# The end of a convolution layer: row order, early weights' pieces, and a product with adding transfers

## The chip, the cores and the metric

The kernel runs on one core of a Trainium2 chip. Its engines work side by side, each through its own queue in order: TensorE (PE in the profile; PEld its weight loads), VectorE (DVE), ScalarE (ACT), GpSimd (POOL) and SyncE (SP), which here issues transfers only. The metric is the device time of one launch in microseconds (us), the median of several runs; lower is better.

## The reference

A network of four layers on a sequence of 2048 positions and 640 channels. Layers one and three are a layer norm and a long convolution (a state space kernel, applied by FFT), layers two and four a layer norm and an attention with 32 query heads of 20 channels that share one key and value head. Each adds to the stream.

```python
def _A_ref(u, A_re, A_im, B_re, B_im, C_re, C_im, log_dt, Dskip):
    ...
    K = jnp.einsum("dn,dnl,dn->dl", Cc, P, dB).real
    ...
    Yf = Uf * Kf[None, :, :, :]
    y = irfft2(Yf, ...)[:, :, 0, :L]
    y = y.transpose(0, 2, 1) + u * Dskip[None, None, :]

def _B_ref(x, wq, wk, wv, wo):
    q = (x @ wq).reshape(B, S, H, Dh).transpose(0, 2, 1, 3)
    k, v = x @ wk, x @ wv
    p = _softmax(jnp.einsum("bhqd,bkd->bhqk", q, k) * (Dh ** -0.5))
    return o.transpose(0, 2, 1, 3).reshape(B, S, H * Dh) @ wo

x = A_u
x = x + _A_ref(_layernorm(x), ...)
x = x + _B_ref(_layernorm(x), ...)
x = x + _A_ref(_layernorm(x), ...)
x = x + _B_ref(_layernorm(x), ...)
```

## The kernel before

`tile_layers` runs a generation of the convolution kernels (`kgen`), then `conv_layer("a")`, `attn_layer("b")`, `conv_layer("c")` and `attn_layer("d")`. The stream x (2048 x 640) stays in SBUF as a tile of 128 partitions by 16 rows ("tau") by 640 channels. A row here is one tau: 128 positions by 640 channels. `TAUS` lists the 16 rows in four groups of four, by the order in which the inverse transform gives them.

**A convolution layer** goes through the channels in five chunks of 128 (`c` = 0 to 4). A chunk is normalised on ScalarE (L818), transformed by matmuls with a table of cosines and sines (L652, `raw` and `dense`), then by butterflies of length 8 on VectorE (`whole`, `fft8`, L114 and L117, with scratch B). The spectrum, `A[c]`, holds 16 rows of 256, real parts in the even rows and imaginary parts in the odd ones. It is multiplied by the spectrum of the convolution kernel (`kh`, 2 MB, loaded by SP per chunk, L762), goes through butterflies again and through the inverse matmuls with a table `wi` (L860), four groups g of four rows. An inverse writes one of two PSUM banks (`ps1`), so the third needs the bank of the first, read out. `turn(g)` reads out group g with the addition to x (`residual`: on VectorE at L871, for chunks 0 and 3 on ScalarE at L869, where TensorE has added x itself with an identity matmul, L853) and for g < 2 issues the inverse of group g + 2.

Chunks 0 to 3 are multiplied by `spread`: products in halves of 1024 elements on VectorE (L926, L922, L929, L931), whose sums are made by transfers with addition, issued on POOL's queue (L923, L927). Chunk 4, the last, is multiplied by `product`, six instructions of 2048 elements on VectorE (L837), and goes through `fft8_last`, which gives the inputs of groups 0 and 1 first, in the tile of kh, named K there (the trace calls it Akh), and those of groups 2 and 3 in A (L157, L160). Calls on other engines are woven between these instructions by `weave(calls, between)`, at index numbers of the list: the turns of chunk 3 at 1, 2, 4 and 5 and the weights' pieces at 3 + k and 5 + k.

**The weights' pieces** exist in layer a only. The projection weights are split into a high and a low part (wh, wl), six pieces: k = 0 for wk and wv, k = 1 to 5 for 128 rows of wq each. `first(k)` loads a piece (L1031), rounds it on ScalarE (L1036) and forms the rest on TensorE (L1038, L1040) in one of three PSUM tiles of two banks (`ps2`), `second(k)` writes the rest out on ScalarE (L1045); after the last, wh and wl are stored (L1048) for layer d's use, where layer c loads them.

**The next norm.** The statistics of channels 0 to 383 of all rows are taken on ScalarE during chunk 3 (`stats_first`, L692 to L696, scratch in the tile xn, named xnas or xncs), those of channels 384 to 639 on VectorE when the last chunk's residual of a group is done (`stats_last`, L708, L710). `stats_base` (L701) and `norm_part` (L724 to L731, with `root`, L736 to L741) merge them: first for group 0, then for groups 1 to 3. The root is on ScalarE, the rest on VectorE. All of this from the last `turn(0)` on is outside the block of `manual_schedule`, so that a planner orders it, by program order and estimated times; within such a block the order on the named engines is that of the program.

**The attention layer** begins with `prepare(0)`: four rows of the first block are normalised on ScalarE (L1105, tiles x), transposed on TensorE (L1114), split into xh on ScalarE (L996) and xl on VectorE (L999), in three steps of two, two and one column blocks. `project` multiplies them by wh and wl (L1131), 15 matmuls for each of six parts. Its tiles lie in the memory that the convolution layer frees, tile by tile: a tile waits for the last reader of what lay there. At the same point POOL clears vt, ones and kt (L1075 to L1082), and VectorE casts ob (L1086).

Of the kernel before, what the change touches and what calls it, by code (L numbers as in the profile page):

```python
# [11 lines left out]
F32 = mybir.dt.float32  # L12
# [135 lines left out]
def fft8_last(nc, A, B, R, K):  # L148
# [13 lines left out]
    tt(A[:, 0:8], B[:, 0:8], B[:, 8:16], ADD)  # L162
# [6 lines left out]
    tt(A[:, 8:16], B[:, 0:8], B[:, 8:16], SUB)  # L169
# [24 lines left out]
class Net:  # L194
# [508 lines left out]
    def stats_last(self, g):  # L703

        nc = self.nc
        st = self.xp.tile([P, 4, 6], F32, tag="st", bufs=2, name=f"sl{g}")
        for n in range(4):
            nc.vector.bn_stats(st[:, n], self.x[:, TAUS[4 * g + n], NA:D])  # L708
        for n in range(4):
            nc.vector.bn_aggr(self.mvb[:, 4 * g + n], st[:, n])  # L710
# [5 lines left out]
    def norm_part(self, g, n):  # L716
# [7 lines left out]
        tt(ed, shift, mean, ALU.add)  # L724
        stt(ve, var, PB, base, op0=ALU.mult, op1=ALU.add)
        stt(sq, ed, PA * PB, ed, op0=ALU.mult, op1=ALU.mult)
        stt(nm, ed, -PB, shift, op0=ALU.mult, op1=ALU.add)
        tt(ve, ve, sq, ALU.add)
        rs = self.rs[:, gs]
        self.root(ve, sq, rs)  # L730
        tt(self.nmr[:, gs], nm, rs, ALU.mult)  # L731

    def root(self, ve, sq, out):

        nc = self.nc
        nc.scalar.activation(sq, ve, AF.Sqrt)  # L736
        nc.vector.reciprocal(out, sq)
        nc.vector.tensor_tensor(sq, out, out, ALU.mult)
        nc.vector.tensor_tensor(sq, sq, ve, ALU.mult)
        nc.vector.tensor_scalar(sq, sq, -0.5, 1.5, ALU.mult, ALU.add)  # L740
        nc.vector.tensor_tensor(out, out, sq, ALU.mult)  # L741

    def norm(self, nm, g):
# [10 lines left out]
        self.root(ve, sq, rs)  # L754
# [35 lines left out]
    def conv_layer(self, nm, first):  # L790
# [7 lines left out]
        with tc.manual_schedule(engines={mybir.EngineType.PE, mybir.EngineType.Activation,  # L798
# [37 lines left out]
            def product(A, kh):  # L836
                return [lambda a=a: tt(*a) for a in (  # L837
                    (m(B, 0), m(A, 0), m(kh, 0), ALU.mult),
                    (R, m(A, 1), m(kh, 1), ALU.mult),
                    (m(B, 0), m(B, 0), R, ALU.subtract),  # L840
                    (m(B, 1), m(A, 0), m(kh, 1), ALU.mult),
                    (R, m(A, 1), m(kh, 0), ALU.mult),
                    (m(B, 1), m(B, 1), R, ALU.add))]
# [22 lines left out]
            def residual(c, g, y):  # L866
# [5 lines left out]
                if c == NCH - 1:  # L872
                    self.stats_last(g)
# [65 lines left out]
            for c in range(NCH):  # L939
                A = As.pop(c)  # L940
                if c == NCH - 1:
                    late = [(1, lambda turn=turn: turn(0)), (2, lambda turn=turn: turn(1)),
                            (4, lambda turn=turn: turn(2)), (5, lambda turn=turn: turn(3))]
                    late = sorted(late + [(3 + k, a[0]) for k, a in enumerate(pieces)]
                                  + [(5 + k, a[1]) for k, a in enumerate(pieces)], key=lambda a: a[0])
                    K = khs.pop(c)
                    weave(product(A, K) + fft8_last(nc, A, B, R, K), late)
                else:
# [10 lines left out]
                    if c == NCH - 2:  # L959
                        scr = new_xn("s").rearrange("p a d -> p (a d)")  # L960

                        def dump(n):
                            return scr[:, 1280 + NA * (n % 4) : 1280 + NA * (n % 4) + NA]

                        self.stats_setup(nm)
                        for g in range(4):
                            self.stats_first(g, dump)
                        pieces = self.attn_weights(scr, nm == "a")
# [9 lines left out]
        turn(0)  # L978
        self.stats_base()
        self.norm_part(0, 1)  # L980
        for g in range(1, 4):
            turn(g)
        self.norm_part(1, 3)
# [8 lines left out]

    def split(self, hi, lo, src, act=False):
        nc = self.nc
        if act:
            nc.scalar.activation(hi, src, AF.Copy)  # L996
        else:
            nc.vector.tensor_copy(hi, src)
        nc.vector.tensor_tensor(lo, src, hi.bitcast(F32), ALU.subtract)  # L999

    def attn_weights(self, scr, fresh):
# [17 lines left out]
        minus = scr[:, 2816:2944]  # L1019
# [6 lines left out]
        def first(k):  # L1026
            hi = ends(k)[0]
            pw = pws[k] = self.ps2(f"pw{k}")
            if k:
                src = scr[:, D * (k % 2) : D * (k % 2) + D]  # L1030
# [39 lines left out]
    def _attn(self, ctx, nm, out):  # L1070
# [20 lines left out]
        with tc.tile_pool(name=f"pj{nm}", bufs=1, reuse_waits="tile") as pj:  # L1091
# [5 lines left out]
            xhs, xls = {}, {}  # L1097
# [370 lines left out]
```

## Time and profile before

| | us |
|---|---|
| median of 3 runs | 3002.05 (3000.38 to 3004.14) |
| profiled execution | 2999.59 |
| its span | 2997.8 |
| busy: TensorE, ScalarE, VectorE | 2777.6, 2426.4, 1378.1 |
| last chunk of layer a: first instruction of `product` to first projection matmul | 571.43 to 620.26 |
| the same of layer c | 1876.83 to 1923.07 |

The profile is that of one execution. Its page gives sums per engine and per group of instructions; the answers of the trace give the instructions in order of time. A row of the timeline reads: start, length, engine, line of the kernel, operation, written tile <- read tiles, shapes, how many were merged; in brackets the idle time of the engine just before it, and what ended it. Start times are us from the span's start. TensorE's granted clock is 0.956 of full speed on the mean.

### The profile page before, as it was taken

The numbers are of one execution on the slowest core, as the hardware profiler recorded it, in microseconds if no ns is written. First come the engines' busy times: TensorE is split into PE (matmuls) and PEld (weight loads), VectorE is DVE, ScalarE is ACT, GpSimd is POOL, SyncE is SP. The second block draws the span as 40 slices with busy tenths as digits, with TensorE's granted clock in tenths as the row PEclk, the third lists the DMA queues.
The fourth block names the chain that finished last, engine by engine and source line by source line (L and its number), as shares of the span: only waits on it lengthen the run. The fifth ranks groups of instructions, "written<-read, shape, count | busy, mean of one in ns | idle before, by whom it ended". The sixth has DMA issues, their size and how long they took to land. (4 is left out here: it accounts for less than half of the span.)

```text
span 2997.8 us, 52536 instructions
## 1 busy us (share of the span) xinstructions
PE 2777.6 (93%) x21712; PEld 1269.2 (42%) x21712; DVE 1378.1 (46%) x1794; ACT 2426.4 (81%) x2904; POOL 86.7 (3%) x149
## 2 busy tenths in 40 slices
PE   2776989898999999999999998898999999999999
PEld 0333978775232333232333687772233333333333
DVE  7999899942122332322232599722222322222222
ACT  5888243444999999999999634338999999999997
POOL 0001001000000000000000011000000000000000
PEclk9855999999999999999999999899999999999999
DMA  6113555433200000001000256131001101110100
GB/s 145 34 19 100 186 162 113 104 114 113 81 22 25 22 25 22 27 21 28 21 26 20 87 113 160 39 129 51 22 25 26 39 21 28 38 26 24 41 19 23
DMA packets 126000, 175.60 MB, mean 59 GB/s; under 512 B 59460, under 2 KB 81988, under 8 KB 122132
## 3 DMA queue, kind: packets, MB, share of 16 engines
q1 hardware_dynamic: 102680, 137.70, 15.8%
q0 software_dynamic: 21104, 33.45, 5.5%
q8 instruction: 175, 2.87, 0.4%
q10 hardware_dynamic: 1968, 0.98, 0.1%
q14 instruction: 73, 0.60, 0.1%
HBM read 95.22 MB, written 48.04 MB: 48 GB/s over the span
## 5 line engine op out<-in xcount | busy, mean ns | idle before, releaser
L1264 ACT ACTIVATE pt<-scb 128x1024 f32<-128x1024 f32 x1024 | 942.2, 1113 | 6.7 <-PE scb L1260 5.1
L1264 ACT ACTIVATE pt<-scd 128x1024 f32<-128x1024 f32 x1024 | 942.1, 1115 | 5.8 <-DMA qpd<-mxd 3.9
L1274 PE MATMUL pob<-pt,vt 128*32 128x512 f32 x4096 | 546.6, 606 | 4.4 <-DVE on L1291 0.2
L1274 PE MATMUL pod<-pt,vt 128*32 128x512 f32 x4096 | 546.3, 605 | 4.4 <-DVE on L1291 0.2
L1260 PE MATMUL scb<-qpb,kt 62*128 62x512 f32 x2048 | 385.8, 451 | 6.0 <-DVEq L1209 5.6
L1260 PE MATMUL scd<-qpd,kt 62*128 62x512 f32 x2048 | 385.4, 451 | 5.6 <-DVEq L1209 5.2
L1260 PEld LDWEIGHTS scb<-qpb,kt 62*128 62x128 f32 x2048 | 166.0, 185 | 401.4 <-ACT pt L1264 392.0
L1260 PEld LDWEIGHTS scd<-qpd,kt 62*128 62x128 f32 x2048 | 165.8, 184 | 401.1 <-ACT pt L1264 392.2
L1322 DVE TENSOR_TENSOR x<-pyd,x 128x320 f32<-128x320 f32 x146 | 71.8, 491 | 560.9 <-PE pyd L1334 560.9
L1322 DVE TENSOR_TENSOR x<-pyb,x 128x320 f32<-128x320 f32 x146 | 71.8, 492 | 547.4 <-PE pyb L1334 547.4
L1294 DVE RECIPROCAL rc<-rc 128x512 f32<-128x512 f32 x62 | 207.9, 3353 | 2.1
L1274 PEld LDWEIGHTS pob<-pt,vt 128*32 128x32 f32 x4096 | 80.6, 108 | 178.1 <-issue 160.0
L1274 PEld LDWEIGHTS pod<-pt,vt 128*32 128x32 f32 x4096 | 80.6, 108 | 177.6 <-issue 159.5
L1334 PE MATMUL pyb<-wo,ot 128*32 128x320 f32 x1168 | 105.3, 432 | 0.0
L1334 PE MATMUL pyd<-wo,ot 128*32 128x320 f32 x1168 | 105.3, 432 | 0.0
L652 PE MATMUL za<-xna,wf 128*128 128x256 f32 x384 | 87.4, 390 | 5.0 <-ACT xna L818 5.0
L652 PE MATMUL zc<-xnc,wf 128*128 128x256 f32 x384 | 85.8, 385 | 5.0 <-ACT xnc L818 5.0
L860 PE MATMUL ya<-Aa,wi 128*128 128x128 f32 x576 | 71.8, 289 | 15.5 <-DVE Aa L114 15.5
L1291 DVE COPY on<-pod 128x512 f32<-128x512 f32 x31 | 21.4, 691 | 134.6 <-PE pod L1274 120.6
L1291 DVE COPY on<-pob 128x512 f32<-128x512 f32 x31 | 21.4, 691 | 133.0 <-PE pob L1274 110.0
L443 PE MATMUL pe<-kg,tm 48*128 48x512 bf16 (+1 forms) x120 | 60.1, 603 | 23.9 <-ACT m L451 15.4
L652 PEld LDWEIGHTS za<-xna,wf 128*128 128x128 f32 x384 | 74.8, 196 | 16.8 <-ACT xna L818 6.2
(367 smaller groups left out, 3204.2 us busy)
## 6 DMA issues: line engine op xcount, KB each, us to landing
Akh<-kh SPq DMA_DIRECT2D x10, 2048.0 KB
kh<-Ak SPq DMA_DIRECT2D x5, 2048.0 KB
qhd<-qh SPq DMA_DIRECT2D x40, 256.0 KB
qld<-ql SPq DMA_DIRECT2D x40, 256.0 KB
qpb<-qhd SPq DMA_DIRECT2D x256, 40.0 KB
qpd<-qhd SPq DMA_DIRECT2D x256, 40.0 KB
ot<-on SPq DMA_DIRECT2D x216, 40.0 KB
wf<-in_c_wf POOLq DMA_DIRECT2D x16, 512.0 KB, 7.9
```

The source lines that it names most:

```text
L443: nc.tensor.matmul(pe[:, 512 * h : 512 * h + 512], grp(tm, u, par, rows), kg[0:rows, col : col + 512], start=True, stop=True)
L652: nc.tensor.matmul(zv[:, :, c, kk], self.wf[:, t + 4 * h, j, c, kk], x, start=(n == 0), stop=(n == 3))
L860: nc.tensor.matmul(y[:, s * DC : (s + 1) * DC], self.wi[:, t, j, c_, kk], v[:, 2 * t + c_, kk], start=(i == 0 and not whole), stop=(i == 3 ...
L1260: nc.tensor.matmul(sc[:, 512 * par : 512 * par + 512], kt[rows, 128 * t : 128 * t + 128], qps[nb, hg, pr][rows], start=True, stop=True)
L1264: nc.scalar.activation(pt, sc, AF.Exp, scale=SCALE)
L1274: nc.tensor.matmul(po[32 * j : 32 * j + 32], vt[:, t], pts[step, j // 2][:, 512 * (j % 2) : 512 * (j % 2) + 512], start=(t == 0), stop=(t ...
L1291: nc.vector.tensor_copy(on, po)
L1294: nc.vector.reciprocal(rc, rc)
L1322: nc.vector.tensor_tensor(xh, py, xh, ALU.add)
L1334: nc.tensor.matmul(py[j : j + m], o[:, 128 * i + j : 128 * i + j + m], w[:, 320 * half : 320 * half + 320], start=start, stop=stop)
```

## The change

It does these things:

- `product` takes the imaginary part first, in two halves of 1024 elements: A1 x K0 into B1, A0 x K1 into R, and a transfer with addition on POOL's queue adds R to B1. Then the real part: A0 x K0 into B0, A1 x K1 in place into K1, the difference into B0. Six whole instructions become four halves and three wholes: one of VectorE's six lengths is left out.
- `fft8_last` begins with the even rows (real parts), sum and difference, then the sum of the odd rows; the difference of the odd rows stays behind K.
- In layer a the pieces 0 to 3 are issued ahead of `stats_first` and so ahead of chunk 3's inverses, their second steps between the groups of `stats_first`; the pieces 4 and 5 stay woven in, at 6 to 9. Sources take three places in the scratch instead of two, dumps two instead of four.
- From the last chunk's `turn(0)` on, the order is written out (the block of `manual_schedule` goes on): `turn(0)` ahead of the last two butterflies, then `stats_base`, the statistics of group 0, the first half of its norm, `turn(1)`, the statistics of group 1 with the second half of that norm woven in, and so on. `norm_part` and `root` return lists of calls.
- `prepare(0)` of the attention is in a written order too: the norm of groups 1 to 3 stands on VectorE and ScalarE around the first xl. The tile xh of block 0 is allocated first, ahead of the tiles x, and xh has two names instead of two buffers of one name.

```diff
-    tt(A[:, 0:8], B[:, 0:8], B[:, 8:16], ADD)
+    tt(A[:, 0:8:2], B[:, 0:8:2], B[:, 8:16:2], ADD)
+    tt(A[:, 8:16:2], B[:, 0:8:2], B[:, 8:16:2], SUB)
+    tt(A[:, 1:8:2], B[:, 1:8:2], B[:, 9:16:2], ADD)
     tt(R[:, 0:4], A[:, 0:4], A[:, 4:8], ADD)
...
-    tt(A[:, 8:16], B[:, 0:8], B[:, 8:16], SUB)
+    tt(A[:, 9:16:2], B[:, 1:8:2], B[:, 9:16:2], SUB)
...
             def product(A, kh):
-                return [lambda a=a: tt(*a) for a in (
+                calls = []
+                for h in range(2):
+                    s = slice(4 * h, 4 * h + 4)
+
+                    def imag(s=s):
+                        tt(R[:, s], m(A, 0)[:, s], m(kh, 1)[:, s], ALU.mult)
+                        nc.gpsimd.dma_start(m(B, 1)[:, s], R[:, s], accum_op=ALU.add)
+
+                    calls += [lambda s=s: tt(m(B, 1)[:, s], m(A, 1)[:, s], m(kh, 0)[:, s], ALU.mult), imag]
+                return calls + [lambda a=a: tt(*a) for a in (
                     (m(B, 0), m(A, 0), m(kh, 0), ALU.mult),
-                    (R, m(A, 1), m(kh, 1), ALU.mult),
-                    (m(B, 0), m(B, 0), R, ALU.subtract),
-                    (m(B, 1), m(A, 0), m(kh, 1), ALU.mult),
-                    (R, m(A, 1), m(kh, 0), ALU.mult),
-                    (m(B, 1), m(B, 1), R, ALU.add))]
+                    (m(kh, 1), m(A, 1), m(kh, 1), ALU.mult),
+                    (m(B, 0), m(B, 0), m(kh, 1), ALU.subtract))]
...
-                    late = sorted(late + [(3 + k, a[0]) for k, a in enumerate(pieces)]
-                                  + [(5 + k, a[1]) for k, a in enumerate(pieces)], key=lambda a: a[0])
+                    late = sorted(late + [(6 + k, a[0]) for k, a in enumerate(pieces[4:])]
+                                  + [(8 + k, a[1]) for k, a in enumerate(pieces[4:])], key=lambda a: a[0])
                     K = khs.pop(c)
-                    weave(product(A, K) + fft8_last(nc, A, B, R, K), late)
+                    calls = product(A, K) + fft8_last(nc, A, B, R, K)
+                    weave(calls[:-2], late)
...
                         self.stats_setup(nm)
+                        pieces = self.attn_weights(scr, first)
+                        for a in pieces[:4]:
+                            a[0]()
                         for g in range(4):
                             self.stats_first(g, dump)
-                        pieces = self.attn_weights(scr, nm == "a")
+                            for a in pieces[max(g - 1, 0) : (0, 1, 2, 4)[g]]:
+                                a[1]()
...
-        turn(0)
-        self.stats_base()
-        self.norm_part(0, 1)
-        for g in range(1, 4):
-            turn(g)
-        self.norm_part(1, 3)
+            turn(0)
+
+            for call in calls[-2:]:
+                call()
+            self.stats_base()
+            for g in range(4):
+                if g > 0:
+                    turn(g)
+                among = part[6:] if g == 1 else ()
+                weave(self.stats_last(g), [(min(n + 1, 8), a) for n, a in enumerate(among)])
+                if g == 0:
+                    part = self.norm_part(0, 1)
+                    for call in part[:6]:
+                        call()
...
-                src = scr[:, D * (k % 2) : D * (k % 2) + D]
+                src = scr[:, D * (k % 3) : D * (k % 3) + D]
...
-            xhs, xls = {}, {}
+            xhs, xls = {0: pj.tile([P, 5, 512], F32R, tag="xh0", bufs=1, name="xh0")}, {}
...
-                xh = xhs[nb] = pj.tile([P, 5, 512], F32R, tag="xh", bufs=2, name=f"xh{nb}")
+                if nb > 0:
+                    xhs[nb] = pj.tile([P, 5, 512], F32R, tag=f"xh{nb % 2}", bufs=1, name=f"xh{nb}")
+                xh = xhs[nb]
...
-                    self.split(xh[:, k0 : k0 + n], xl[:, k0 : k0 + n],
-                               pt[:, 0 : 512 * n].rearrange("p (k c) -> p k c", k=n), act=True)
+                    hi, lo = xh[:, k0 : k0 + n], xl[:, k0 : k0 + n]
+                    pv = pt[:, 0 : 512 * n].rearrange("p (k c) -> p k c", k=n)
+                    nc.scalar.activation(hi, pv, AF.Copy)
+
+                    def low(hi=hi, lo=lo, pv=pv):
+                        nc.vector.tensor_tensor(lo, pv, hi.bitcast(F32), ALU.subtract)
+
+                    weave([low], [(0 if n < 6 else 1, a) for n, a in enumerate(
+                        self.norm_part(1, 3) if nb == k0 == 0 else ())])
...
-            prepare(0)
+            with tc.manual_schedule(engines={mybir.EngineType.Activation, mybir.EngineType.DVE}):
+                prepare(0)
```

52 lines of the change are left out of this document (22 added, 30 removed).

## The prediction

> **What bounds the kernel now.** First the page, for the span; then the timeline of each engine around the place that the diff touches.
>
> ```profile
> span 2997.8 us, 52536 instructions
> ```
>
> The two convolution layers (tiles named a and c) end with the last channel chunk, and behind each stands an attention layer whose projections keep TensorE busy from then on. So what counts is when the first projection matmul starts. The timeline of VectorE at the end of layer a (start, length, line, tile, number of instructions), at the product, at the butterflies and at the first residual:
>
> ```profile
> 571.43 2.29 DVE L837 TENSOR_TENSOR B<-Aa,Akh 128x2048 f32<-128x2048 f32 x1
> 573.64 2.29 DVE L837 TENSOR_TENSOR Ra<-Aa,Akh 128x2048 f32<-128x2048 f32 x1
> ```
> ```profile
> 587.33 2.36 DVE L157 TENSOR_TENSOR Ra<-Aa 128x1024 f32<-128x1024 f32 x2
> 589.61 2.49 DVE L157 TENSOR_TENSOR Akh<-Ra 128x512 f32<-128x512 f32 x4
> 592.02 2.28 DVE L157 TENSOR_TENSOR Aa<-B 128x2048 f32<-128x2048 f32 x1
> 594.34 2.50 DVE L157 TENSOR_TENSOR B<-Aa 128x512 f32<-128x512 f32 x4
> ```
> ```profile
> 598.19 2.50 DVE L160 SCALAR_TENSOR_TENSOR Aa<-B 128x512 f32<-128x512 f32 x4
> 600.61 0.68 DVE L871 TENSOR_TENSOR x<-ya,x 128x512 f32<-128x512 f32 x1
> 601.39 1.41 DVE L708 BATCH_NORM_STATS2 sl<-x 128x6 f32<-128x256 f32 x4
> 602.72 0.36 DVE L710 BATCH_NORM_AGGREGATE mvba<-sl 128x2 f32<-128x6 f32 x4
> ```
>
> No row names idle time: VectorE runs through. The inputs of the first two inverses (Akh) are there from 590.2 (the first of four instructions) to 592.1. TensorE's timeline, and further down the first projection:
>
> ```profile
> 595.22 1.25 PE L1040 MATMUL pw<-wh,xnas 128*128 128x512 f32 x4
> 596.30 7.31 PE L860 MATMUL ya<-Akh,wi 128*128 128x128 f32 x64
> 603.45 7.31 PE L860 MATMUL ya<-Aa,wi 128*128 128x128 f32 x64
> ```
> ```profile
> 620.26 0.43 PE L1131 MATMUL pqb<-xh,wh 128*52 128x512 f32 x1 [1.35 <-DVE xl L999]
> ```
>
> It stands in the weights' pieces (pw) until 596.30, 6 us past its first input. The four inverses then take 14.46 us, and ScalarE waits for their end:
>
> ```profile
> 610.85 0.92 ACT L1105 ACTIVATE x<-x,nmrna,rsna 128x640 f32<-128x640 f32 x1 [5.21 <-PE ya L860]
> 613.86 0.21 ACT L736 ACTIVATE sq<-ve 128x12 f32<-128x12 f32 x1 [2.09 <-DVE ve L728]
> 613.98 2.53 ACT L1105 ACTIVATE x<-x,nmrna,rsna 128x640 f32<-128x640 f32 x3
> 617.92 2.43 ACT L996 ACTIVATE xh<-ptb 128x1024 fp32r<-128x1024 f32 x3 [1.42 <-PE ptb L1114]
> ```
>
> One normalised row comes out, then the root for the other twelve stands in front of the next three. In layer c there are no pieces; the same places there, on VectorE, TensorE, ScalarE and TensorE:
>
> ```profile
> 1895.02 2.49 DVE L157 TENSOR_TENSOR Akh<-Rc 128x512 f32<-128x512 f32 x4
> ```
> ```profile
> 1902.57 0.69 DVE L871 TENSOR_TENSOR x<-yc,x 128x512 f32<-128x512 f32 x1 [0.33 <-PE yc L860]
> ```
> ```profile
> 1895.81 10.30 PE L860 MATMUL yc<-Akh,wi 128*128 128x128 f32 x64 [6.49 <-issue]
> ```
> ```profile
> 1913.34 0.92 ACT L1105 ACTIVATE x<-x,nmrnc,rsnc 128x640 f32<-128x640 f32 x1 [3.00 <-PE yc L860]
> ```
> ```profile
> 1923.07 0.43 PE L1131 MATMUL pqd<-xh,wh 128*52 128x512 f32 x1 [1.09 <-DVE xl L999]
> ```
>
> The starts to beat are 620.26 and 1923.07.
>
> **The change, part by part.** *Product.* Before, from 571.43 to the first Akh at 589.61: 18.18 us. After: four halves of 1.14 (half of the R pair's 2.28) are 4.56; then 2.21 (start to start, independent), 2.29 and 2.29: 11.35. Even rows' sum and difference 2.28, odd rows' sum 1.14, R pair 2.28: 17.05. Akh starts 1.13 us earlier: 588.48 in a, 1893.89 in c. One 2.29 us instruction goes, but the difference of the even rows now stands ahead of Akh. Behind it: Akh 2.41, odd difference 1.14, six butterflies 3.85 (594.34 to 598.19), two of the four L160 1.21: the first residual 8.61 after Akh.
>
> *Adding transfers.* The sum of the imaginary halves goes to POOL's queue. The nearest rows are those of `spread`, with four transfers of the same 512 KB; on VectorE, on POOL, and the landing times of L927 and of L923:
>
> ```profile
> 533.93 2.35 DVE L926 TENSOR_TENSOR Aa<-Aa,Akh 128x1024 f32<-128x1024 f32 x2
> 536.20 2.35 DVE L922 TENSOR_TENSOR Aa<-Aa,Akh 128x1024 f32<-128x1024 f32 x2
> ```
> ```profile
> 535.68 2.58 POOL L927 DMA_DIRECT2D Aa<-Ra  x2 [34.41 <-issue]
> ```
> ```profile
> DMA to landing us min/median/max: 6.0/7.3/14.1
> ```
> ```profile
> DMA to landing us min/median/max: 10.4/12.2/17.4
> ```
>
> POOL starts 0.55 us after the first half of L926 ends (535.1). So the second add is issued 5.2 us after the product's start, and the odd rows' sum, which needs it, stands at 13.63: 8.4 us to land. L927 are the first two of four, L923 queue behind them. Two alone are like the first pair: I take 7.3, hidden by the three real-part instructions and the even rows. Bounds 6.0 and 17.4; past 8.4 it costs one for one, in both layers, since the whole rest of the layer is queued behind that sum on VectorE. L922 shows that VectorE goes on in the interleaved rows of a tile while an add into it is under way.
>
> *Pieces.* Four of six move ahead of the fourth chunk's inverses, ScalarE's part of them ahead of its statistics. The idle time there on TensorE and ScalarE; the DMA engines in a window (last two columns: share, GB/s); SP's queue:
>
> ```profile
> 564.58 6.76 PE L860 MATMUL ya<-Aa,wi 128*128 128x128 f32 x32 [9.98 <-DVE Aa L114]
> ```
> ```profile
> 571.37 0.60 ACT L869 ACTIVATE x<-ya 128x512 f32<-128x512 f32 x1 [8.02 <-PE ya L860]
> ```
> ```profile
> 552.00:554.00 2.00, 2.00 (x17) 1.77 (x16) 1.61 (x4) 2.00 (x9) 0.00 (x0) 1.00 0.32 39
> ```
> ```profile
> 553.54 0.34 SPq L762 DMA_DIRECT2D Akh<-kh  x1
> ```
> ```profile
> 594.72 0.33 SPq L1048 DMA_DIRECT2D whd<-wh  x1
> ```
>
> TensorE idles 9.98 us there, ScalarE 8.02. By the 1.25 row a full piece (two such groups) is 2.3 us of TensorE; four with the small one are about 8 us, on ScalarE about 5. ScalarE's first piece waits for its loads, with all statistics queued behind it. The window says that the loads of that place are nearly through by 554; with the third one (320 KB more) I put 555. SP issues them ahead of the 2 MB for Akh (553.54), which then share the engines; the product needs Akh only at 571.43. The stores of the finished weights (594.72) leave some 6 us sooner, when the adds have landed. The fourth piece needs the bank of the first, which ScalarE empties only behind two groups of statistics, and the inverses stand behind it: they may slip a few us. But TensorE is needed free, with the pieces 5 and 6 done, at 589.1 only. I count 0. If that cover goes, each us past 589.1 delays the inverses, to at most the old 596.30.
>
> *End of the layer.* Rows that size the norms (VectorE), the memsets on POOL, and the group of L740 (least, median and greatest ns):
>
> ```profile
> 613.24 0.17 DVE L724 TENSOR_TENSOR ed<-smshifta,mvba 128x12 f32<-128x12 f32 x1
> ```
> ```profile
> 615.19 0.17 DVE L731 TENSOR_TENSOR nmrna<-nm,rsna 128x12 f32<-128x12 f32 x1
> ```
> ```profile
> 618.98 2.95 DVE L999 TENSOR_TENSOR xl<-ptb,xh 128x1024 fp32r<-128x1024 f32 x3 [3.35 <-ACT xh L996]
> ```
> ```profile
> 604.66 2.79 POOL L1082 MEMSET kt<- 1x1536 f32 x2
> ```
> ```profile
> L740 DVE TENSOR_SCALAR sq<-sq x4: 134/172/970, 606.5 to 1917.6; 128x4 f32<-128x4 f32 x2, 128x12 f32<-128x12 f32 x2
> ```
>
> Five small instructions before the root take 0.62 (613.24 to 613.86), six behind it 1.29 (614.07 to 615.36), a group's statistics 1.69 (601.39 to 603.08). One L740 took 0.97 where the median is 0.17; it began at 606.5 and ended with POOL's memsets (607.45). These start when Akh (a) or B (c) is free, and now fall beside the one-input instruction of `stats_base`: I charge 0.7 in a and 0.3 in c, bounds 0 and 1.4 (one memset) each. [...]
>
> Layer a: first residual 597.09, done 597.77; two L160 598.98; `stats_base` with the 0.7, 599.85; statistics 601.54; five small 602.16; second residual 602.84; statistics with six small ones woven in (0 to 1.29, I take 0.4 up to nmr) 604.95. TensorE: inverses one and two 589.1 to 596.4; the third when the first residual has freed its bank, to 601.4; the fourth when the second has (602.84), to 606.5. The rows x leave the memory that the inverses read (xh0 is put there), so they start with nmr at 604.95; without the root between them they take 0.92 + 2.53, to 608.40. From there as before: xh 1.41 later (616.51 to 617.92), xl 1.06, projections 1.28: 612.15. VectorE is by then through the fourth statistics and five small ones (610.5), in time for xl at 610.87. New is that six small ones, 1.29, stand between the first xl and the second; TensorE has matmuls to cover part, I charge 0.6 (0 to 1.29): 612.75, gain 7.5.
>
> Layer c, by the same steps: first residual 1902.50 (TensorE's first inverse is over by 1902.57 - 1.13), 1903.18, 1904.39, 1904.86 with the 0.3, 1906.55, 1907.17, 1907.85, nmr 1909.95; x to 1913.40; xh 1914.81; xl 1915.87 (VectorE free at 1915.5); projections 1917.15 + 0.6: gain 5.3.
>
> Sum -12.8 us. The profiled run took 2999.59, 1.8 more than its span: 2986.8. The median of the runs shown, 3002.05 (3000.38 to 3004.14), is 2.4 above it: **2989.2**.
>
> **The rivals.**
> *x still waits for the last inverse.* 606.5 instead of 604.95 and 1912.2 (1913.34 - 1.13) instead of 1909.95: 3.8 less, 2993.0. For it: both L1105 rows show exactly this wait, and the trace shows no addresses. Against: xh0 is as large as the four x together.
> *The pieces hold TensorE up all the same.* Inverses as before, last end 610.76; xl 613.8 behind the last statistics, projections 615.7: gain 4.6 in a, 2992.1. For: ScalarE is in order and its first piece waits for loads. It decides from 589.1 on.
> *The adds land late.* With 12.2, 3.8 a layer: 2996.8. With 17.4, 9.0 a layer: 18.0 against 12.8, 3007.3, **slower**. A landing of 14.8 turns the sign, 17.8 makes it more than 0.2%. For: the second landing row. Against: two adds, not four, and nothing else is under way there.
> *The gain is lost in the projections*, whose order is left to the planner. TensorE's waits for xl in them (sum, times):
>
> ```profile
>   DVE xl L999: 16.0, 16
> ```
>
> If these double, 16.0 us go: 3005.2. Against: their code is the same.
>
> **How the numbers follow.** Forecast 0.64; x waits 0.08; pieces 0.09; late adds 0.11 (0.03 slower by over 0.2%); projections 0.08 (0.02 slower by over 0.2%). The forecast's own range: charges at their lower ends 3.0 better, at their upper ends 5.0 worse, 2.5 for the scatter of runs: 2983.7 to 2996.7. With the others 2983.0 to 2998.0. A measurement of this kernel can tell 0.2%, 6 us, from no change. Faster by more: 0.64 + 0.08 + 0.09 and 0.02 of the late adds, 0.83; slower 0.05; the rest, 0.12, within.
>
> **What would show it.** Akh 17.0 us after the product, and no wait of VectorE for a DMA ahead of the odd rows' sum. TensorE's inverses directly behind Akh in a. Four x in one go, released by VectorE, not TensorE. First projection matmuls near 612.8 and 1917.8, if the start of the product stays. It would be wrong if the pieces 5 and 6 ended past 589.1, if ScalarE's statistics began later than 556, or if the waits for xl in the projections grew.

## The result, and the profile after

The changed kernel takes 2985.87 us (median of 4 runs, 2983.20 to 2988.15), beside 3002.34 (3000.38 to 3004.14) for the kernel before: a ratio of 0.9949, 95% interval 0.9937 to 0.9960. The profiled execution took 2985.19. One of the six launches of e11 below took 4232.98 us at a mean granted clock of 0.588, and is left out of its median. All line numbers below are those of the kernel whose profile is shown.

The first line of the page, then VectorE's timeline in layer a, from the product's first instruction to the first residual (start, length, line, written tile <- read tiles), and the rows of layer c for the two ends:

```profile
span 2983.4 us, 52547 instructions
```
```profile
569.49 1.22 DVE L848 TENSOR_TENSOR B<-Aa,Akh 128x1024 f32<-128x1024 f32 x1
...
580.87 3.50 DVE L157 TENSOR_TENSOR Aa<-B 128x1024 f32<-128x1024 f32 x3
...
586.68 2.49 DVE L157 TENSOR_TENSOR Akh<-Ra 128x512 f32<-128x512 f32 x4
...
595.41 0.68 DVE L880 TENSOR_TENSOR x<-ya,x 128x512 f32<-128x512 f32 x1
```
```profile
1866.81 1.22 DVE L848 TENSOR_TENSOR B<-Ac,Akh 128x1024 f32<-128x1024 f32 x1
...
1892.73 0.68 DVE L880 TENSOR_TENSOR x<-yc,x 128x512 f32<-128x512 f32 x1
```

Akh comes 17.19 us after the product's start, the first residual 25.92, in both layers. The three instructions at 580.87, the third of which needs the adds, follow one another without a bracket: VectorE does not wait for the adding transfers. Then ScalarE's rows x and TensorE's first projection matmuls, a and c:

```profile
602.88 3.36 ACT L1117 ACTIVATE x<-x,nmrna,rsna 128x640 f32<-128x640 f32 x4 [3.09 <-DVE nmrna L732]
...
610.19 0.43 PE L1152 MATMUL pqb<-xh,wh 128*52 128x512 f32 x1 [2.34 <-DVE xl L1135]
...
612.49 0.43 PE L1152 MATMUL pqb<-xl,wh 128*52 128x512 f32 x1 [0.24 <-DVE xl L1135]
```
```profile
1899.76 3.36 ACT L1117 ACTIVATE x<-x,nmrnc,rsnc 128x640 f32<-128x640 f32 x4 [2.64 <-DVE nmrnc L732]
...
1906.48 0.43 PE L1152 MATMUL pqd<-xh,wh 128*52 128x512 f32 x1 [1.89 <-DVE xl L1135]
```

All four rows x go in one run of 3.36 us, and what released them is nmr of VectorE, where it was TensorE's last inverse before. From the product's start to the first projection matmul, layer a now takes 610.19 - 569.49 = 40.70 us (48.83 before), layer c 39.67 (46.24 before): 8.13 and 6.57 less, 14.70 together. The span is 14.4 shorter. What is left over is the rest of the program, which differs from run to run: over the traces below, the start of layer a's product lies between 569.26 and 572.32, the stretch from the first projection of layer b to the product of layer c is 1255.5 to 1257.8 long, and that from the first projection of layer d to the end 1074.7 to 1078.0 (the 1074.7 is the one trace of the kernel before; the others begin at 1075.5). The experiments change tenths to a few us, so they are read from the two intervals, in one profiled execution each, and not from the time.

### The profile page after: what moved, and what is told of

Its sections match the earlier page's. It is cut to its first block, busy times and chain, and to the rows that moved or that the text cites. A ratio compares the mean times of both kernels' runs of the same rounds, so it can differ in the third digit from the quotient of the medians.

```text
span 2983.4 us, 52547 instructions
## 1 busy us (share of the span) xinstructions
PE 2774.5 (93%) x21712; PEld 1262.1 (42%) x21712; DVE 1373.9 (46%) x1800; ACT 2425.9 (81%) x2904; POOL 91.6 (3%) x153
## 5 line engine op out<-in xcount | busy, mean ns | idle before, releaser
L654 PEld LDWEIGHTS zc<-xnc,wf 128*128 128x128 f32 x384 | 73.7, 193 | 16.4 <-ACT xnc L821 6.2
```

Source lines behind the costliest of these rows:

```text
L654: nc.tensor.matmul(zv[:, :, c, kk], self.wf[:, t + 4 * h, j, c, kk], x, start=(n == 0), stop=(n == 3))
```

## The experiments

Each starts from the changed kernel. All in one table, intervals in us (product's first instruction to first projection matmul); the time is a median where there are more runs than one. The times come from several chips, on which single runs of the kernel before took 2997.8 to 3005.0, so differences of a few us in that column say nothing:

| | layer a | layer c | time |
|---|---|---|---|
| before | 48.83 | 46.24 | 3002.34 |
| changed kernel | 40.70 | 39.67 | 2985.87 |
| the same again | 40.80 | 39.67 | 2986.77 (5 runs) |
| e1 pieces as before | 43.08 | 39.66 | 2989.28 |
| e2 product as before | 41.73 | 41.73 | 2991.01 |
| e3 place of xh as before | 43.06 | 41.20 | 2987.74 |
| e4 norm ahead of the rows x | 45.65 | 44.84 | 2995.61 |
| e5 sums on VectorE | 42.18 | 42.19 | 2990.30 |
| e6 first piece written out earlier | 40.82 | 39.67 | 2987.71 |
| e7 one add twice | 43.49 | 44.21 | 2996.46 |
| e8 written order and xh's place alone | 44.48 | 41.73 | 2991.87 |
| e10 two groups of statistics first | 39.68 | 39.68 | 2987.07 |
| e11 e10, small norm instructions later | 39.68 | 39.68 | 2988.06 (5 runs) |
| e12 e10, TensorE filled | 39.66 | 39.65 | 2983.73 (5 runs) |

**e1: the pieces.**

```diff
-                    late = sorted(late + [(6 + k, a[0]) for k, a in enumerate(pieces[4:])]
-                                  + [(8 + k, a[1]) for k, a in enumerate(pieces[4:])], key=lambda a: a[0])
+                    late = sorted(late + [(6 + k, a[0]) for k, a in enumerate(pieces)]
+                                  + [(8 + k, a[1]) for k, a in enumerate(pieces)], key=lambda a: a[0])
...
-                        for a in pieces[:4]:
-                            a[0]()
...
```

> Only the place of the weights' pieces goes back: all six are formed and written beside the last chunk's product and butterflies, as before. What counts is the interval from the product's first instruction to the first projection matmul; with the change it was 40.70 us in layer a and 39.67 in layer c. Theory (early pieces free TensorE for the last inverses): TensorE is held until about 25 us after the product's start, the four inverses end some 3 us later, and layer a's interval grows by 2.5 to 3.5, to 43.2 to 44.2. Rival (VectorE alone sets the end, the place of the pieces is of no account): 40.7 to 41.0. Layer c has no pieces: 39.7 by both.

Layer a grew by 2.38 (just under the range given), layer c by nothing. The inverses start when TensorE is through the pieces, and VectorE's first residual now waits for them, 27.88 after the product instead of 25.92. That is 1.96 of the 2.38; the rest is the small instruction of L742, which takes 1.00 beside POOL's memsets instead of 0.60 (see below):

```profile
593.67 7.31 PE L869 MATMUL ya<-Akh,wi 128*128 128x128 f32 x64
597.44 0.69 DVE L880 TENSOR_TENSOR x<-ya,x 128x512 f32<-128x512 f32 x1 [1.87 <-PE ya L869]
```

**e2 and e5: the product.** e2 puts back the six whole instructions and the old beginning of `fft8_last`:

```diff
...
+                return [lambda a=a: tt(*a) for a in (
                     (m(B, 0), m(A, 0), m(kh, 0), ALU.mult),
-                    (m(kh, 1), m(A, 1), m(kh, 1), ALU.mult),
-                    (m(B, 0), m(B, 0), m(kh, 1), ALU.subtract))]
+                    (R, m(A, 1), m(kh, 1), ALU.mult),
+                    (m(B, 0), m(B, 0), R, ALU.subtract),
+                    (m(B, 1), m(A, 0), m(kh, 1), ALU.mult),
+                    (R, m(A, 1), m(kh, 0), ALU.mult),
+                    (m(B, 1), m(B, 1), R, ALU.add))]
...
```

e5 keeps the new order and only takes the transfers away:

```diff
-                        nc.gpsimd.dma_start(m(B, 1)[:, s], R[:, s], accum_op=ALU.add)
+                        tt(m(B, 1)[:, s], m(B, 1)[:, s], R[:, s], ALU.add)
```

> Only the product and the first instructions of the last butterflies go back: six whole instructions on VectorE, no adding transfers, whole first sum and difference. Theory (VectorE's chain from the product to the first residual sets the end): Akh comes 18.2 us after the product's start instead of 17.2, the first residual some 2.0 later, so layer c grows by 1.8 to 2.2, to 41.5 to 41.9, and layer a by about 1.6, since TensorE held the inverses 0.5 there anyway: 42.1 to 42.6. Rival (the end waits for TensorE or for a transfer, VectorE has slack): no change, 40.7 and 39.7.

> Only the adding transfers go: the two halves of the imaginary sum are formed on VectorE (two more instructions of 1.14 us), the new order stays. Theory (what the product gives is the work taken off VectorE by the transfers; the new order by itself gives nothing): layer c grows by 2.2 to 2.4, to 41.9 to 42.1, a little over the 41.73 of the old product; layer a comes to the same 41.9 to 42.1, since what delays it beside layer c (TensorE and the memsets) is hidden by a slower VectorE. Rival (the order, imaginary part and even rows first, is what gives): growth under 1.2 in layer c, under 40.9.

e2 cost 2.06 in layer c, as expected, and 1.03 in layer a, less than expected: with a later VectorE all that made layer a longer than layer c is gone, both are 41.73. e5 cost 2.52 in layer c, 0.1 above its range, and came out at 42.2, 0.46 longer than the old product. So the order by itself gains nothing (it costs 0.46), and all of the 2.06 comes from the sum's two instructions that the transfers took off VectorE.

**e3: the place of xh.**

```diff
-            xhs, xls = {0: pj.tile([P, 5, 512], F32R, tag="xh0", bufs=1, name="xh0")}, {}
+            xhs, xls = {}, {}
...
-                if nb > 0:
-                    xhs[nb] = pj.tile([P, 5, 512], F32R, tag=f"xh{nb % 2}", bufs=1, name=f"xh{nb}")
-                xh = xhs[nb]
+                xh = xhs[nb] = pj.tile([P, 5, 512], F32R, tag="xh", bufs=2, name=f"xh{nb}")
```

> Only the place in memory goes back: the tile xh of the first block is no longer allocated ahead of the normalised rows x. Theory (x then lies on what the last inverses read, and waits for them): the row x on ScalarE is released by TensorE's last inverse instead of by the factor nmr of VectorE; layer a grows by about 2.2, to 42.5 to 43.2, and layer c by 1.6 to 1.9, to 41.2 to 41.6. Rival (the allocation is of no account, the written order alone lets the rows go): 40.7 and 39.7, still released by nmr.

Layer a grew by 2.36, layer c by 1.53, to the lengths expected. The rows x of a and c have another releaser in their brackets:

```profile
606.79 3.36 ACT L1117 ACTIVATE x<-x,nmrna,rsna 128x640 f32<-128x640 f32 x4 [6.19 <-PE ya L869]
...
1903.53 3.35 ACT L1117 ACTIVATE x<-x,nmrnc,rsnc 128x640 f32<-128x640 f32 x4 [4.34 <-PE yc L869]
```

This is a wait that no line of the code asks for: which tile is allocated first decides whether ScalarE waits for TensorE. (The trace shows no addresses; what it shows is the releaser, which goes with the allocation.)

**e4: the norm of groups 1 to 3.**

```diff
+            for call in self.norm_part(1, 3):
+                call()
...
-                        self.norm_part(1, 3) if nb == k0 == 0 else ())])
+                        ())])
```

> Only the place of the norm for groups 1 to 3 goes back: it stands at the end of the convolution layer, its root on ScalarE ahead of the first four rows x, its small instructions on VectorE ahead of the first xl. Theory (the rows x then wait for the last group's statistics): layer a grows by 5 to 6, to 45.7 to 46.7, layer c by 4.7 to 5.7, to 44.4 to 45.4; the stall of TensorE behind the first projection matmuls (0.41) goes. Rival (xl waits for VectorE's last statistics anyway, so that only the root's place on ScalarE counts): under 2 a layer, 41 to 42.7 and 40 to 41.7.

4.95 in layer a and 5.17 in layer c: the largest single part (a hair under the range in a). The rows x are split again, one alone and three behind the root, and TensorE's transposes wait for them. The stall of 0.41 is gone in layer a (3.50 from the first to the sixteenth start of the projection matmuls); in layer c, at 5.46, a lower clock (0.57 in the 5 us behind the first of them) hides it:

```profile
602.62 0.92 ACT L1119 ACTIVATE x<-x,nmrna,rsna 128x640 f32<-128x640 f32 x1 [3.04 <-DVE nmrna L732]
...
608.63 2.53 ACT L1119 ACTIVATE x<-x,nmrna,rsna 128x640 f32<-128x640 f32 x3
609.59 3.79 PE L1130 MATMUL ptb<-ident,x 128*128 128x128 f32 x17 [3.85 <-ACT x L1119]
```

**e7: how late the adds may land.**

```diff
+                        for _ in range(1 + s.start // 4):
                             nc.gpsimd.dma_start(m(B, 1)[:, s], R[:, s], accum_op=ALU.add)
```

> The adding transfer of the product's second half is issued twice, so the imaginary part of those rows gets its second product two times over, which the reference doesn't have; nothing else is changed. Theory (the odd rows' sum, 13.66 us after the product's start, needs the last add, and everything behind it is queued on VectorE): the last of the three adds lands later than 13.66, at 16 to 18.5 by the rows of four adds in a row; VectorE waits for a transfer there, and layer c grows by exactly the length of that wait, 2.3 to 4.9, to 42 to 44.6; layer a by 1.0 less than layer c. Rival (three adds go side by side and still land in time, or the end has other slack): no wait for a transfer, 40.7 and 39.7.

POOL's queue and VectorE in layer c, and the same instruction of VectorE in layer a:

```profile
1878.29 1.28 POOL L847 DMA_DIRECT2D B<-Rc  x1 [0.99 <-DVE Rc L845]
1886.01 1.28 POOL L847 DMA_DIRECT2D B<-Rc  x1 [6.45 <-DMA B<-Rc]
...
1891.56 1.23 DVE L157 TENSOR_TENSOR Ac<-B 128x1024 f32<-128x1024 f32 x1 [4.44 <-DMA B<-Rc]
```
```profile
589.79 1.23 DVE L157 TENSOR_TENSOR Aa<-B 128x1024 f32<-128x1024 f32 x1 [3.72 <-DMA B<-Ra]
```

The third add waits for the second on the same data, lands 5.55 us after its issue, and VectorE's wait of 4.44, within what was expected, comes out as 4.54 in layer c; in layer a 3.72 comes out as 2.79, since 1.03 of VectorE's lateness is hidden there (below). So the price is one for one, as the rival of the late adds had it. The rows also give the margin. The second add was in 7.72 after its issue (1878.29 to 1886.01); it was needed at 1873.37 + 13.66 = 1887.03. In the changed kernel the landing times of the four adds are

```profile
DMA to landing us min/median/max: 5.5/6.5/7.6
```

against the 8.4 of the prediction: the sums are hidden by some 1 us, no more.

**e8: what is left without the pieces and the product.** The edits of e1 and e2 together.

> The pieces are beside the last chunk as before and the product is the old one; what stays of the change is the written order of rows, statistics and norms and the place of xh. Theory (the parts add up where they act on the same chain and hide each other where they don't): layer c as with the old product alone, 41.7; in layer a the late pieces hold TensorE until about 25 to 26 us and the old product holds VectorE until 28, so the greater of the two counts: 43.0 to 44.0 (against 41.73 with the old product alone, 43.08 with late pieces alone). Rival (the two costs add in full): 44.1 to 44.6. By this the written order with xh's place is the largest part: 48.83 to 43.5 in layer a and 46.24 to 41.7 in layer c.

Layer c as expected, layer a 44.48, above the theory's range and within the rival's. The traces say why, and it is not the rival. The inverses of chunk 3, ahead of the pieces, began at a lower clock: over their 32 matmuls it was 0.55 in e8 (first row), as in the kernel before, and 0.72 in e1 (second row):

```profile
562.51 6.71 PE L861 MATMUL ya<-Aa,wi 128*128 128x128 f32 x32 [9.98 <-DVE Aa L114]
```
```profile
562.83 5.19 PE L869 MATMUL ya<-Aa,wi 128*128 128x128 f32 x32 [9.97 <-DVE Aa L114]
```

So TensorE was through the pieces 25.51 after the product's start in e8 and 24.11 in e1, 1.40 later; 43.08 + 1.40 = 44.48. The greater of the two costs counts, and TensorE's was greater by its clock. Of the 8.13 and 6.57, the written order with xh's place alone gives 4.35 and 4.51.

**e6 and e10: why layer a is 1.03 longer than layer c.** The pieces should have been free of charge in layer a, but TensorE came to the last inverses only 21.72 us after the product's start, nearly 4 after the first of Akh was ready (17.99 in e10, below). My first reading was the fourth piece, which waits for the first one's bank (changed kernel):

```profile
564.21 2.50 PE L1050 MATMUL pw<-xnas,ident 128*128 128x512 f32 x4 [6.72 <-ACT wl L1057]
...
591.21 7.31 PE L869 MATMUL ya<-Akh,wi 128*128 128x128 f32 x64
```

e6 writes the first piece out right behind the forming of the third:

```diff
                         for a in pieces[:4]:
                             a[0]()
+                            if a is pieces[2]:
+                                pieces[0][1]()
```

> One step is moved in layer a: the first piece is written out right behind the forming of the third, so that the fourth finds a free bank and chunk 3's inverses start as soon as VectorE gives their inputs. Theory (the 1.03 us by which layer a's interval is longer than layer c's are TensorE's: the fourth residual waits 0.47 for it, the transposes stand behind the fourth inverse, the memsets come late and meet a small VectorE instruction): layer a falls from 40.70 to that of layer c, 39.6 to 39.8. Rival one (only the 0.47 is TensorE's): 40.2. Rival two (TensorE has room enough): 40.7. Rival three (TensorE alone sets the end): by 2 or more, under 38.7. Layer c: 39.67 by all.

A miss: 40.82, nothing gained. Two of chunk 3's inverses did start early, but the third waited for the bank that ScalarE's residual frees, and that came as late as before:

```profile
577.43 1.07 ACT L878 ACTIVATE x<-ya 128x512 f32<-128x512 f32 x2
578.06 2.08 PE L862 MATMUL ya<-x,ident 128*128 128x512 f32 x2 [5.08 <-ACT x L878]
```

ScalarE's row has no bracket: it was busy up to there. Its queue begins with a wait for the first piece's loads, and all four groups of statistics stand behind it (changed kernel):

```profile
551.99 0.42 ACT L1048 ACTIVATE wh<-kv 128x260 fp32r<-128x260 f32 x1 [13.10 <-DMA kv<-in_B_wk]
...
575.41 0.58 ACT L878 ACTIVATE x<-ya 128x512 f32<-128x512 f32 x1
```

So e10 puts two groups of statistics into that wait, with e6's order of the pieces behind them (it was not run without e6's order):

```diff
-                        for a in pieces[:4]:
-                            a[0]()
                         for g in range(4):
                             self.stats_first(g, dump)
-                            for a in pieces[max(g - 1, 0) : (0, 1, 2, 4)[g]]:
+                            if g == 1:
+                                for k, a in enumerate(pieces[:4]):
+                                    a[0]()
+                                    if k == 2:
+                                        pieces[0][1]()
+                            for a in pieces[(1, 1, 1, 2)[g] : (0, 0, 2, 4)[g]]:
                                 a[1]()
```

> In layer a two of the four groups of statistics on ScalarE stand ahead of the first pieces, where ScalarE now idles 13.10 us for the first piece's loads. Theory (not the fourth piece's bank but ScalarE's queue holds chunk 3's inverses: its first residual comes 5.9 us after the product's start, and behind it the pieces 5 and 6 and the last inverses): that residual comes within 1 us of the product's start, chunk 3's inverses end near 13 us after it instead of 16.9, the last inverses start near 18 instead of 21.7, and layer a falls from 40.70 to the length of layer c, 39.6 to 39.8. Rival (the 1.03 between the layers has nothing to do with TensorE): 40.6 to 40.8. Layer c: 39.67 by both.

Layer a is 39.68, layer c 39.68. The wait for the loads is 0.34 instead of 13.10, chunk 3's first residual comes 2.85 us before the product's start (at 570.85) instead of 5.92 behind it, earlier still than expected, and the inverses start with Akh, 17.99 after it (the 2.76 ahead of them is idle time):

```profile
553.39 0.42 ACT L1051 ACTIVATE wh<-kv 128x260 fp32r<-128x260 f32 x1 [0.34 <-DMA kv<-in_B_wk]
568.00 0.60 ACT L878 ACTIVATE x<-ya 128x512 f32<-128x512 f32 x1 [0.66 <-PE ya L869]
```
```profile
588.84 7.38 PE L869 MATMUL ya<-Akh,wi 128*128 128x128 f32 x64 [2.76 <-issue]
```

e6's order alone gained nothing, so that settles the 1.03: it was ScalarE's queue, by way of TensorE. Yet the time of e10 (one run) is no better than the changed kernel's.

**e11 and e12: the stall behind the first projection matmuls, and their clock.** e11 adds to e10 the moving of the last six small norm instructions behind the second xl (its expectation says the third), and of the cast of ob behind `prepare(0)` in the program; the planner left the cast where it was, ahead of the first xl, so that part wasn't tried.

```diff
...
-                    weave([low], [(0 if n < 6 else 1, a) for n, a in enumerate(
-                        self.norm_part(1, 3) if nb == k0 == 0 else ())])
+                    if nb == k0 == 0:
+                        rest = self.norm_part(1, 3)
+                        for call in rest[:6]:
+                            call()
+                    low()
+                    if nb == 0 and k0 == 2:
+                        for call in rest[6:]:
+                            call()
...
```

> The same with two more moves in both layers: the six small norm instructions behind the third xl instead of the first, and the cast of ob behind all of prepare(0). Theory: the cast holds the first xl by 0.2 and the small ones hold TensorE by 0.41 just after the first projection matmuls; both go. The interval is 39.4 to 39.5 in both layers and the stall of 0.4 behind the first column block is gone: 1.7 less in layer a and 0.6 less in layer c than the changed kernel, 2.3 together, 2983.5 against 2985.9 within the scatter of runs of some 2.5. Rival (the moved instructions make the second block's rows x late and TensorE waits there): the waits for xl in the projections grow and no time is won.

> The changed kernel as it is, beside the one above on the same chip: 2983 to 2989 by both theories, with intervals of 40.70 and 39.67 as before.

e11 is a miss: the intervals stay at 39.68 in both layers. No wait for xl is seen behind the first projection matmuls, but none in e10 either, where the matmuls themselves are slower; so what the move is worth isn't shown. In time nothing is won, 2988.06 beside 2986.77 on the same chip (0.9954, 0.9941 to 0.9967, beside 0.9950, 0.9938 to 0.9963). In both layers the first 15 projection matmuls took 5.07 us from the first start to the sixteenth, as in e10 (5.06 and 5.08), where they took 3.96 and 3.95 in the changed kernel with the stall and 3.5 in the kernel before. The windows of 5 us ahead of and behind the first projection matmul of layer a (busy time of PE, PEld, DVE, ACT, POOL, the granted clock, DMA share, GB/s), in e10 and in the changed kernel:

```profile
605.53:610.53 5.00, 2.58 (x19) 1.80 (x18) 4.93 (x23) 4.08 (x7) 0.00 (x0) 1.00 0.00 0
610.53:615.53 5.00, 5.00 (x15) 2.59 (x16) 2.67 (x8) 3.55 (x5) 0.00 (x0) 0.66 0.00 0
```
```profile
605.19:610.19 5.00, 2.66 (x25) 2.42 (x24) 4.46 (x18) 3.49 (x6) 0.00 (x0) 1.00 0.00 0
610.19:615.19 5.00, 4.76 (x20) 2.76 (x21) 2.67 (x8) 3.98 (x7) 0.00 (x0) 1.00 0.00 0
```

In e10 the clock falls to 0.66 in the 5 us behind the first projection matmul. That costs 1.1 us a layer beside the changed kernel's 3.96, about what e10 had won in layer a. It is no property of e10: in the 12 traces of the changed kernel and its variants up to e11 a lower clock (0.66, in one place 0.57) stands at the first projection matmuls of layer a in 4 and of layer c in 8, in the changed kernel itself in neither layer, in its second trace in layer c. e12 gives TensorE work there:

```diff
+                if nb == 0:
+                    pf = self.ps1(f"pf{nm}")
+                    for i in range(16):
+                        nc.tensor.transpose(pf[:, 128 * (i % 4) : 128 * (i % 4) + 128], xs[3][:, 0:128], self.ident)
```

> The version with two groups of statistics ahead of the pieces, and behind the first block's transposes 16 more transposes of the last row, into a bank that nobody reads, so that TensorE has work until the first projection matmul. It is about the first 15 projection matmuls: in some runs they take 3.95 us from first to sixteenth start, in others 5.07, with eight of them at 0.63 us instead of 0.39 and a granted clock of 0.66 in that stretch. Theory (TensorE's short idle times just ahead of them draw the lower clock onto them): with TensorE filled they take 3.9 to 4.0 in both layers, and the interval from product to first projection matmul stays at 39.7 to 39.9. Rival (the lower clock comes from the idle times farther ahead, among the inverses, or by chance): 5.07 in at least one layer. The time, 2985 to 2988, can't tell one from the other.

```profile
604.05:609.05 5.00, 4.33 (x36) 3.55 (x33) 4.93 (x23) 4.09 (x7) 0.00 (x0) 1.00 0.00 0
609.05:614.05 5.00, 4.75 (x20) 2.76 (x21) 2.67 (x8) 3.98 (x7) 0.00 (x0) 1.00 0.01 3
```

The first 15 matmuls now take 3.96 and 3.94, as expected, the intervals are 39.66 and 39.65, the time is 2983.73 (2982.62 to 2987.45), with a ratio to before of 0.9945 (0.9931 to 0.9958). That is the lowest median of all versions, but its runs overlap those of the changed kernel and were made on another chip than those of e10, e11 and the changed kernel's second series, so a gain over the change isn't shown. Nor is the cause of the lower clock settled: two stretches at the full clock, where about half of 24 had it before, come by chance about one time in four.

## Why the prediction was right, point by point

Predicted were 2989.2 and a gain of 12.8 us; the time was 2985.87, within the range, and the two intervals gave 14.70.

- *Product.* Akh 17.05 after the start was 17.19. That the odd rows' sum would not wait held; 7.3 for the landing was between the median and the greatest of the four, and e7 shows the price past the margin. Right.
- *First residual.* Forecast 25.66 after the product (597.09 - 571.43), measured 25.92 in both layers: 0.26 too early.
- *Rows x.* They follow nmr, not the last inverse (e3), and go in one piece (e4). Forecast 33.52 (a) and 33.12 (c) after the product, measured 33.39 and 32.95. The path is right. That the size in layer a is right too is partly luck: the 0.7 charged at `stats_base` was not paid, and made up for the 0.26 of the first residual and for 0.44 further on (below) that was not forecast there.
- *Pieces at no cost.* The mechanism was right, since e1 shows 2.38 gained by moving them. The step that was mis-sized is "TensorE is needed free, with the pieces 5 and 6 done, at 589.1 only. I count 0": that is 17.67 after the product, and TensorE was free at 21.72. The slip was on ScalarE, whose first piece waits for its loads with all statistics queued behind it; the prediction said so, and bounded TensorE's delay only by "a few us" of the fourth piece's bank. By the prediction's own signs this part came out wrong: the pieces 5 and 6 ended 4 us past that time, and the inverses of layer a did not follow directly behind Akh. The price stayed small because VectorE came to the first residual only at 25.92, and had no wait there. It cost 1.03 by e10, in three places that the two layers' rows tell apart: nmr 0.44 later, the first xh 0.15 later behind rows x (1.00 of idle time instead of 0.85), and 0.45 for VectorE, whose fourth residual waits for TensorE.
- *Small instructions beside POOL's memsets.* Charged were 0.7 and 0.3 at `stats_base`, an estimate from the one long L740 (0.97 instead of 0.17); there it met none, and took 0.17 in both layers. In layer a it was met further on, by the group of L742, whose result the very next small instruction needs (least, median, greatest ns):

```profile
599.56 2.79 POOL L1094 MEMSET kt<- 1x1536 f32 x2
```
```profile
L742 DVE TENSOR_SCALAR sq<-sq x4: 153/173/601, 601.8 to 1907.0; 128x4 f32<-128x4 f32 x2, 128x12 f32<-128x12 f32 x2
```

  One of four took 0.60 instead of 0.17 and ended when the memsets did (602.38 and 602.35): that is the 0.44. In six other traces (the second of the changed kernel, e1, e3, e4, e6, e8) the same instruction of layer a took 0.56 to 1.01 us, and each time ended 0.02 or 0.03 behind the memsets. So the term was 0.44 and 0 instead of 0.7 and 0.3, and its place was wrong too: in e5 the instruction of `stats_base` did meet a memset and took 1.29 (at 600.71), but the statistics behind it began 0.08 later and ran their 1.40 as ever, and nmr came at 35.20 after the product, as in layer c (35.21). In these two traces a held instruction cost something only where the next one needs its result. The 0.44 is less than a whole memset, since L742 began late in the two: at 601.78, where they ran from 599.56 to 602.35.
- *xh, xl, projections.* From the last row x to the first projection matmul 3.75 were forecast; 3.95 in a and 3.36 in c were measured. Nearly half of the gain in c that the forecast missed is here: the wait of 1.41 for the first xh was 0.85, as the transposes of the first rows run beside the later rows x. Against it stands the cast of ob, 0.35 long, ahead of the first xl, which the forecast did not have; it holds xl for about 0.2 in c.
- *Stall among the projection matmuls.* Charged 0.6, measured 0.41 in each layer (the first 15 matmuls take 3.96 from first to sixteenth start, where they took 3.5).

By layers the forecast gains of 7.5 and 5.3 were 8.13 - 0.41 = 7.7 and 6.57 - 0.41 = 6.2. Of the 3.3 between 2989.2 and 2985.87, 1.1 are these and 0.5 lie elsewhere in the program. The other 1.7 are the run on which the sum was made: the median of before lay 2.4 above its profiled execution and that was added, while that of the changed kernel lies only 0.7 above its own.

The rivals: the rows x do wait for the last inverse if xh lies elsewhere (e3), and the change moves it. The pieces do hold TensorE up, by 4 us instead of none, of which 1 us came through. The adds are 1 us from being late. The waits for xl in the projections, whose growth was to be a sign of being wrong, did grow from 16.0 us in 16 waits:

```profile
  DVE xl L1135: 21.5, 20
```

This row adds the waits of the weight loads to those of the matmuls. The matmuls' own were 6.6 before (3.4 and 3.2) and are 8.9 now (4.6 and 4.3), so the price of 16.0 us in that rival was set too high. Of the 2.3 more, 1.8 lie ahead of the first projection matmul (2.34 and 1.89 instead of 1.35 and 1.09), inside the intervals, and 0.5 are the two stalls. So nothing more is seen to be lost in the projections' order; what the end of the program lost or gained by the change, with one trace of before, is not shown.

## What to carry to other kernels

Parts that shorten the same chain do not add up: undone one by one (e1 to e4) they cost 10.7 us in layer a, together they gave 8.1. What a part is worth depends on the others that are in, and taking it out of the finished version tells what it is worth there. When work with loads moves to the front of an in-order queue, look at what stands behind it there: the wait for the load, 13.10 us here, passes to all of it. Other work put into that wait cost nothing in e10: the wait was then 0.34, and layer a 1.02 shorter. And where two engines are within a us of each other, read which tile lies where a tile still in use was, and how far each hidden transfer is from its reader: here the first was worth 2.36 and 1.53 us, and the second has 1 us to spare.

## What was not expected of the hardware

TensorE's granted clock falls to 0.66 over 5 us at the start of the projections in 11 of the 24 places, though TensorE was idle for no more than 2.4 us at a time in the 12 us before. (In a twelfth, layer c of e4, it had waited 4.63 us, and the clock was at 0.50 already ahead of the projections.) How busy TensorE was just before does not tell the places apart: in layer c it was busy for 2.85 of the last 5 us in e1, e10 and the changed kernel's second trace, where the clock fell, and for 2.51 to 2.58 in e3, e5 and e7, where it stayed full. The slower matmuls follow each other at 0.43 us instead of 0.23, for some 3.3 us. What brings the lower clock on there, no run here shows.

The clock also accounts for what looked like a cost of e8: 32 inverse matmuls take 6.7 us in one trace (granted clock 0.55) and 5.2 in another (0.72) behind the same 10 us of idle time, and 3.73 at the full clock (layer c of the changed kernel, at 1867.30): length times clock is 3.69, 3.74 and 3.73.
